# Down-projection of a gated decode kernel with batch rows as outputs: 72 wide matmuls instead of 144 narrow ones, fewer VectorE instructions, last output weights split by columns

## The chip, the cores and the metric

The kernel runs on one core of one Trainium2 chip. The metric is the device time of one execution in microseconds (us).

## The reference

```python
g = sigmoid((x * gate_w).sum(-1))                        # x: 8 x 1 x 576
q = (x @ wq).reshape(8, 1, 32, 128)                      # 32 heads of 128
a = softmax(q . k_cache / sqrt(128)) . v_cache           # caches: 8 x 32 x 4096 x 128
a = a.reshape(8, 1, 4096) @ wo
b = gelu(layernorm(x) @ w1 + b1) @ w2 + b2               # w1: 576 x 4608, w2: 4608 x 576
return g * a + (1 - g) * b                               # everything bf16 in memory
```

The two caches are nearly all of the 557 MB that must be read. The second branch (b) is small, but its weights are read first and it is computed first.

## The kernel before

SBUF has three big slots. The loads go, in order, wq, w1, w2 into slots 0, 1, 2, then K0, K1, V0, K2, V1, K3, V2, ... (8 MB each; a number is a group of 8 heads of one batch row), each into the slot of three loads earlier. A load may therefore be issued only when its slot's previous content has been used: K1 after the up-projection (w1), V0 after the down-projection (w2), K2 after the scores of group 0 (K0), and V1 after the scores of group 1 (K1). All issues come from one queue, in this order.

```python
    def load_kv(kind, g):
        n = n_load[0]; n_load[0] += 1
        s = n % 3
        ...
        land[kind, g] = op("sync", lambda e: e.dma_start(slot[s][:, :, :], src), free[n - 3], dma=dma)

    # down-projection: the 576 output columns as four quarters of 144 at partition offsets 0, 32, 64, 96
    def quarters(lhsT, w, first, stop, waits):
        for i in range(4):
            last = op("tensor", lambda e, i=i: e.matmul(
                y_ps[32 * i:32 * i + B, 0:QN], lhsT=lhsT, rhs=w[:, i * QN:(i + 1) * QN], start=first, stop=stop),
                waits if i == 0 else ())
        return last

    for jt in range(NJ):                                   # NJ = 36 k tiles
        p_down = quarters(hT_sb[:, jt, :], w2_sb[:, jt, :], jt == 0, False, ...)
    for i in range(4):
        p_b2 = ...                                         # (1 - g) * b2, fp32, into the same y_ps
    free[2] = [p_b2]
    ...
    def q_of(g):        # mask q on GpSimd, broadcast it by two matmuls, copy it on ScalarE
    def mult(g, c):     # VectorE: K chunk *= q; then TensorE adds the products up into PSUM
    def scores(g, between):
        mult(g, 0); between(0); mult(g, 1); between(1)
        for c in range(NCK):                               # 8 chunks
            reduce(g, c)                                   # VectorE, from PSUM
            if c + 2 < NCK: mult(g, c + 2); between(c + 2)
```

In TensorE's program the q broadcast of group 0, and with it all scores, stands behind the down-projection (at 59.22 us before the change, behind the last matmuls of that branch at 58.86).

## Time and profile before

| | before |
|---|---|
| median | 1296.31 us (three runs, known when the prediction was made); 1295.85 us with the three runs made beside the changed kernel |
| mean read rate | 431 GB/s |
| DMA queue q1, share of the 16 engines' span | 99.6% |
| TensorE, VectorE, ScalarE busy | 57%, 63%, 12% |

From the page of the kernel before: the busy time of each engine over the span, the read rate in 40 equal slices of the span, and the main DMA queue.

```profile
PE 733.4 (57%) x4926; PEld 337.1 (26%) x4926; DVE 819.7 (63%) x873; ACT 161.0 (12%) x587; POOL 40.4 (3%) x60
GB/s 406 427 447 424 439 430 436 432 430 436 434 428 436 436 432 438 430 438 432 430 436 434 428 436 438 430 438 430 438 430 432 436 432 434 432 438 430 436 424 366
q1 hardware_dynamic: 10528, 556.94, 99.6%
```

No engine is near full; the reads are at nearly the same rate, 424 to 447 GB/s, in every slice but the first and the last. The kernel is a stream of loads, and an engine matters only where it lets that stream run dry, or after the last landing.

The timeline of the kernel before, cut to what gates the early loads. Columns: start and length in us, engine, line, operation, what it writes and reads, count, and in brackets the idle time before it and what ended it. SL is the memory of the slots and all that is cut from them, PS is PSUM. SPq rows are the load issues.

```profile
42.96 0.33 SPq L384 DMA_DIRECT2D SL<-in_A_k_cache_dram  x1
...
54.97 3.96 PE L544 MATMUL PS<-SL 128*8 128x144 bf16 x144 [2.07 <-DVE SL L538]
58.86 0.43 PE L553 MATMUL PS<-SL,diag 8*8 8x144 f32 x8
59.22 0.25 PE L569 MATMUL PS<-Qm,Sel 128*64 128x128 bf16 x2
59.34 0.33 SPq L384 DMA_DIRECT2D SL<-in_A_v_cache_dram  x1
...
59.89 4.49 DVE L580 TENSOR_TENSOR SL<-SL,q_bc 128x4096 bf16<-128x4096 bf16 x2 [5.06 <-DMA SL<-in_A_k_cache_dram]
...
84.42 0.33 SPq L384 DMA_DIRECT2D SL<-in_A_k_cache_dram  x1
...
111.47 0.33 SPq L384 DMA_DIRECT2D SL<-in_A_v_cache_dram  x1
```

Read downward: 144 matmuls in 3.96 us, 27 ns each (a sign of overlap: the 384-column matmuls of the up-projection, one after another, start 163 ns apart at the full clock, which is 61 ns for 144 columns; the profile also records the clock that TensorE is granted, here 0.5 or 1.0 of full speed, "cold" and "warm" in the prediction), then b2, then the q broadcast, then the first score multiply at 59.89 us. The issues are K1, V0, K2 and V1. The packet records of the same trace say when the DMA engines need them: an 8 MB load occupies the engines for 19.35 us, and K2's last packets end between 115.56 and 117.47 us (mean 116.2). V1, issued at 111.47, is thus some 3.7 us ahead of its need, with the time from issue to first packet (about 1 us) taken off. That is the thinnest margin of the kernel: K2, at 84.42, is some 11 us ahead, and by the same sum no later cache load is less than 11 us ahead.

### The profile page before, as it was taken

What the parts mean: (1) busy time and instruction counts of PE and PEld (TensorE: products, weight loads), DVE (VectorE), ACT (ScalarE), POOL (GpSimd) and SP (SyncE); (2) the same over time, 40 slices, a digit from 0 to 9 for tenths busy, and PEclk for the clock granted to TensorE, in tenths of its full rate; (3) what the DMA queues carried; (4) which work ended last, traced back from release to release, by engine and by line L of the source; (5) the groups of instructions that cost most, each with busy time, mean ns of one, the idle gap of its engine ahead of it and who ended that gap; (6) DMA issues with size and microseconds to landing.
All of it is one profiled execution on the core that took longest, in us unless ns stands there. A gap on an engine that the chain in (4) does not pass through costs nothing.

```text
span 1293.2 us, 11790 instructions
## 1 busy us (share of the span) xinstructions
PE 733.4 (57%) x4926; PEld 337.1 (26%) x4926; DVE 819.7 (63%) x873; ACT 161.0 (12%) x587; POOL 40.4 (3%) x60
## 2 busy tenths in 40 slices
PE   3666566555556555556555556555556555556646
PEld 1322223122223222223222223222223222223223
DVE  2387567665567665567665567765567765567762
ACT  1011110111110011110011110011111011111011
POOL 1001000000000000000000000000000000000000
PEclk8799898878898887898787899778888877888888
DMA  9999999999999999999999999999999999999998
GB/s 406 427 447 424 439 430 436 432 430 436 434 428 436 436 432 438 430 438 432 430 436 434 428 436 438 430 438 430 438 430 432 436 432 434 432 438 430 436 424 366
DMA packets 10591, 557.16 MB, mean 431 GB/s; under 512 B 1201, under 2 KB 1233, under 8 KB 1745
## 3 DMA queue, kind: packets, MB, share of 16 engines
q1 hardware_dynamic: 10528, 556.94, 99.6%
q8 instruction: 9, 0.15, 0.0%
q10 hardware_dynamic: 50, 0.04, 0.0%
q14 instruction: 4, 0.03, 0.0%
HBM read 556.96 MB, written 0.01 MB: 431 GB/s over the span
## 4 chain that ended last, share of the span: by engine, by line
DMA 54%; DVE 26%; PE 14%; ACT 5%; issue 1%; SPq 0%; ACTq 0%; DVEq 0%
DMA SL<-in_A_k_cache_dram 50%; DVE SL L580 20%; PE PS L585 7%; DVE s_sb L591 5%; ACT P L625 4%; PE PS L640 4%; DMA SL<-in_B_w_dram 2%; DMA SL<-in_A_wo_dram 2%; PE PS L515 1%; PE PS L656 1%; ACT O_sb L645 1%; PE PS L544 0%; PE PS L518 0%; PE PS L649 0%; PE PS L535 0%
## 5 line engine op out<-in xcount | busy, mean ns | idle before, releaser
L585 PE MATMUL PS<-SL,ident 128*128 128x512 bf16 x2048 | 547.7, 420 | 518.3 <-DVE SL L580 518.3
L580 DVE TENSOR_TENSOR SL<-SL,q_bc 128x4096 bf16<-128x4096 bf16 x256 | 582.0, 2284 | 313.6 <-DMA SL<-in_A_k_cache_dram 313.6
L585 PEld LDWEIGHTS PS<-SL,ident 128*128 128x128 bf16 x2048 | 199.0, 106 | 853.8 <-DVE SL L580 614.8
L591 DVE TENSOR_REDUCE s_sb<-PS 128x32 f32<-128x512 f32 x256 | 175.8, 687 | 90.4 <-PE PS L585 90.3
L625 ACT ACTIVATE P<-s_sb,hb 128x256 bf16<-128x256 f32 x256 | 126.2, 494 | 663.3 <-PE PS L640 645.5
L640 PE MATMUL PS<-SL,P 128*32 128x512 bf16 x2048 | 128.5, 389 | 0.0
L640 PEld LDWEIGHTS PS<-SL,P 128*32 128x32 bf16 x2048 | 96.4, 138 | 17.9 <-issue 3.1
L564 POOL TENSOR_SCALAR Qm<-Q,sel 128x256 bf16<-128x256 bf16 x33 | 33.7, 1020 | 896.6 <-ACT O_sb L645 845.2
L572 ACT ACTIVATE q_bc<-PS 128x128 bf16<-128x128 f32 x33 | 9.1, 277 | 407.4 <-PE PS L569 407.4
L625 ACT ACTIVATION_READ_ACCUMULATOR P<-s_sb,hb 128x1 f32 x256 | 47.7, 186 | 0.0
L656 PE MATMUL PS<-O_sb,selq 128*32 128x128 f32 x256 | 34.2, 278 | 0.7 <-ACT O_sb L645 0.7
L656 PEld LDWEIGHTS PS<-O_sb,selq 128*32 128x32 f32 x256 | 26.0, 113 | 1.4 <-ACT O_sb L645 1.2
L645 ACT ACTIVATE O_sb<-PS 128x512 f32<-128x512 f32 x32 | 18.4, 574 | 10.0 <-PE PS L640 10.0
L523 DVE COPY SL<-PS 104x1152 f32<-104x1152 f32 x1 | 1.4, 1357 | 28.7 <-PE PS L518 28.7
L515 PE MATMUL PS<-SL 128*8 128x384 bf16 x60 | 13.2, 356 | 6.8 <-DMA SL<-in_B_w_dram 6.8
L669 DVE SCALAR_TENSOR_TENSOR On<-PS,rz,dqm 32x128 f32<-32x128 f32 x32 | 10.9, 339 | 9.0 <-PE PS L656 7.9
L683 POOL TENSOR_TENSOR OT<-OTs,g 32x96 bf16<-32x96 f32 (+2 forms) x12 | 4.2, 347 | 320.3 <-DVE OTs L673 320.2
L610 DVE TENSOR_REDUCE mA<-s_sb 128x1 f32<-128x256 f32 x32 | 13.4, 420 | 1.1
L673 DVE TENSOR_REDUCE OTs<-On 32x32 f32<-32x128 f32 x32 | 12.1, 378 | 1.1
L649 PE MATMUL PS<-acc,hsel 128*32 128x8 f32 x64 | 7.4, 188 | 5.9 <-ACT O_sb L645 4.7
L663 DVE TENSOR_REDUCE zs<-PS 32x1 f32<-32x8 f32 x32 | 4.7, 147 | 8.2 <-PE PS L656 7.9
L649 PEld LDWEIGHTS PS<-acc,hsel 128*32 128x32 f32 x64 | 4.5, 110 | 19.5 <-issue 12.7
(82 smaller groups left out, 114.5 us busy)
## 6 DMA issues: line engine op xcount, KB each, us to landing
SL<-in_A_v_cache_dram SPq DMA_DIRECT2D x2, 4096.0 KB, 38.4
SL<-in_B_w_dram SPq DMA_DIRECT2D x1, 5184.0 KB, 37.7
SL<-in_B_w_dram SPq DMA_DIRECT2D x1, 4608.0 KB, 24.1
SL<-in_A_wq_dram SPq DMA_DIRECT2D x1, 4096.0 KB, 13.0
SL<-in_A_wo_dram SPq DMA_DIRECT2D x1, 3456.0 KB, 22.0
SL<-in_A_wo_dram SPq DMA_DIRECT2D x1, 864.0 KB, 23.7
SL<-in_B_w_dram SPq DMA_DIRECT2D x1, 576.0 KB, 25.0
SL<-in_A_wq_dram SPq DMA_DIRECT2D x1, 512.0 KB, 13.6
```

Of the source, the lines that this page charges most:

```text
L515: p_up = op("tensor", lambda e, o=o, r=r, kt=kt, yi=yi: e.matmul(o, lhsT=yT_sb[:, yi, :], rhs=r, start=(kt == 0), stop=False), [v_yT, *ld_ ...
L564: g_qm[g] = op("gpsimd", lambda e: e.tensor_scalar(out=Qm[:, :, :].rearrange("p k d -> p (k d)"), in0=Q4[:, 2 * hg * DH:(2 * hg + 2) * DH] ...
L580: v_mult[g, c] = op("vector", lambda e: e.tensor_tensor(out=part, in0=part, in1=qb, op=ALU.mult), [land["k", g], a_qb[g]], token="tensor" ...
L585: p_sum[g, c] = op("tensor", lambda e, r=r, n=n: e.matmul(tr_ps[par][:, :], lhsT=ident[:, :], rhs=r, start=(n == 0), stop=(n == NCH - 1)), ...
L591: v_red[g, c] = op("vector", lambda e: e.tensor_reduce(out=s_sb[:, c * CT:(c + 1) * CT], in_=tr_ps[par][:, :].rearrange("p (t c) -> p t c" ...
L610: t = op("vector", lambda e: e.tensor_reduce(out=mA[:, 0:1], in_=s_sb[:, :], axis=AX.X, op=ALU.max), [v_red[g, NCK - 1], c_mA], token=own)
L625: a_exp[g] = op("scalar", lambda e, h=h: e.activation(out=P[:, :, h, :], in_=s_sb[:, :].rearrange("p (s t) -> p s t", s=2), func=ACT.Exp, ...
L640: p_pv[g] = op("tensor", lambda e, o=o, lhsT=lhsT, rhs=rhs, tq=tq: e.matmul(o, lhsT=lhsT, rhs=rhs, start=(tq < 4), stop=(tq >= NTQ - 4)), ...
L645: a_ev[g] = op("scalar", lambda e: e.activation(out=O_sb[:].rearrange("p t d -> p (t d)"), in_=o_ps[:, :], func=ACT.Copy), [p_pv[g], p_z.g ...
L649: p_z[g] = op("tensor", lambda e: e.matmul(oz_ps[0:32, DH:DH + HB], lhsT=hsel[:, :], rhs=acc[:, place(g), :], start=True, stop=True), [a_e ...
L656: p_oz[g] = op("tensor", lambda e, tt=tt: e.matmul(oz_ps[0:32, 0:DH], lhsT=selq[:, tt, :], rhs=O_sb[:, tt, :], start=(tt == 0), stop=(tt = ...
L673: v_norm[g] = op("vector", lambda e: e.tensor_reduce(out=OTs[:, :, place(g + 2)], in_=On[:, :].rearrange("p (q j) -> p j q", q=NDQ), axis= ...
```

## The change

Its intent: fewer instructions on TensorE and VectorE, and a shorter end. The down-projection writes the 8 batch rows as one 8 x 576 block, with 512 and 64 columns of w2 moving per k tile; one VectorE instruction of each softmax goes; small copies move from VectorE to ScalarE; the last row of wo comes as two column pieces. The core of the diff (cuts marked):

```diff
+    b_ps = PS[0:B, 5 * 512:5 * 512 + D]
...
     for jt in range(NJ):
-        p_down = quarters(hT_sb[:, jt, :], w2_sb[:, jt, :], jt == 0, False, ...)
+        for n0, n1 in ((0, 512), (512, D)):
+            p_down = op("tensor", lambda e, jt=jt, n0=n0, n1=n1: e.matmul(
+                b_ps[:, n0:n1], lhsT=hT_sb[:, jt, :], rhs=w2_sb[:, jt, n0:n1], start=(jt == 0), stop=(jt == NJ - 1)), ...)
+    v_b = op("vector", ... scalar_tensor_tensor(out=b_sb, in0=b2_8, scalar=1 - g, in1=b_ps, mult, add), [p_down, ld_b2])
     for i in range(4):
-        p_b2 = ... lhsT=diag2[:, 1, :], rhs=b2_f ...
+        p_y = ... lhsT=spread8[:, 0:B], rhs=b_sb[:, i * QN:(i + 1) * QN] ...    # fp32, spreads the rows to the quarters
...
-        t = op("vector", ... mC = -gm ...)
-        t = op("vector", ... transpose(mD, mC))
+        t = op("vector", ... transpose(mD, gmb))           # sign put into the next instruction
...
-    WO = ((0, 24), (24, 30), (30, 32))
+    WO = ((0, 24, 0, 4), (24, 31, 0, 4), (31, 32, 2, 4), (31, 32, 0, 2))
```

More of the change, by code (lines that the diff above doesn't have):

```diff
@@ L268, in bass_gated_mix__mha_block_cached__mixer_channel_mlp__decode_kernel @@
     b2_8 = late.take([B, D])
-    b2_f = late.take32([B, D])
+    b_sb = late.take32([B, D])
     t2 = late.take32([128, FC])
@@ L276, in bass_gated_mix__mha_block_cached__mixer_channel_mlp__decode_kernel @@
     zs = sb("zs", [32, 1], F32)
+    rz = sb("rz", [32, 1], F32)
     acc = sb("acc", [128, GL, HB], F32)
@@ L288, in bass_gated_mix__mha_block_cached__mixer_channel_mlp__decode_kernel @@
     one1 = sb("one1", [1, B], BF16)
-    diag2 = sb("diag2", [B, 2, B], F32)
+    diag = sb("diag", [B, B], F32)
     g4 = sb("g4", [128, 2], F32)
-    g32 = sb("g32", [32, 2, B], F32)
+    g32 = sb("g32", [32, B], F32)
     ident = sb("ident", [128, 128], BF16)
-    hneg = sb("hneg", [128, HB], F32)
+    hpos = sb("hpos", [128, HB], F32)
     sel32 = sb("sel32", [128, HB, TQ], F32)
@@ L298, in bass_gated_mix__mha_block_cached__mixer_channel_mlp__decode_kernel @@
     mB = sb("mB", [128, 32], F32)
-    mC = sb("mC", [128, 32], F32)
     mD = sb("mD", [128, 32], F32)
@@ L304, in bass_gated_mix__mha_block_cached__mixer_channel_mlp__decode_kernel @@
     O_sb = sb("O_sb", [128, TQ, DH], F32)
-    rz = sb("rz", [128, 1], F32)
     PS = nc.alloc_psum_tensor("PS", [128, 8 * 512], F32)
@@ L316, in bass_gated_mix__mha_block_cached__mixer_channel_mlp__decode_kernel @@
     g4_ps = bank[3][:, 0:2]
-    g32_ps = bank[3][0:32, 64:64 + 2 * B]
+    g32_ps = bank[3][0:32, 64:64 + B]
     ht_ps = PS[:, 0:NJ * 32].rearrange("p (j c b) -> p j c b", j=NJ, c=4)
+    b_ps = PS[0:B, 5 * 512:5 * 512 + D]
     xt_ps = bank[7]
@@ L405, in bass_gated_mix__mha_block_cached__mixer_channel_mlp__decode_kernel @@
                                                     base=PH - 1, pattern=[[PH, HB], [0, NDQ]], channel_multiplier=-1), [t])
-    c_hneg = op("vector", lambda e: e.tensor_scalar(out=hneg[:, :], in0=hsel[:, ::NDQ], scalar1=-1.0, scalar2=60000.0,
+    c_hpos = op("vector", lambda e: e.tensor_scalar(out=hpos[:, :], in0=hsel[:, ::NDQ], scalar1=-1.0, scalar2=-60000.0,
                                                     op0=ALU.add, op1=ALU.mult), [c_hsel])
@@ L416, in bass_gated_mix__mha_block_cached__mixer_channel_mlp__decode_kernel @@
         axis=AX.X, op=ALU.add), [c_id])
-    c_selq = op("vector", lambda e: e.tensor_copy(
+    c_selq = op("scalar", lambda e: e.copy(
         out=selq[:].rearrange("p t (h q) -> p t h q", q=NDQ),
@@ L421, in bass_gated_mix__mha_block_cached__mixer_channel_mlp__decode_kernel @@
     c_one1 = memset("gpsimd", one1[:], 1.0)
-    c_b2 = op("gpsimd", lambda e: e.tensor_copy(out=b2_f, in_=b2_8), [ld_b2])
-    c_sp8 = op("vector", lambda e: e.tensor_copy(
+    c_sp8 = op("scalar", lambda e: e.copy(
         out=spread8[:].rearrange("b (c r) -> b c r", c=4),
@@ L427, in bass_gated_mix__mha_block_cached__mixer_channel_mlp__decode_kernel @@
         out=Rows[:], in_=ident[:, :].rearrange("p (h r) -> p h r", h=4), axis=AX.X, op=ALU.add), [c_id])
-    c_Sel = op("vector", lambda e: e.tensor_copy(
+    c_Sel = op("scalar", lambda e: e.copy(
         out=Sel[:].rearrange("p (h r) -> p h r", h=4),
@@ L465, in untransposed @@
     def untransposed(dst, col, waits):
-        return op("vector", lambda e: e.tensor_copy(
+        return op("scalar", lambda e: e.copy(
             out=dst.rearrange("p k b -> p (k b)"), in_=xt_ps[:, col:col + (NKF + 2) * B]), waits)
@@ L476, in bass_gated_mix__mha_block_cached__mixer_channel_mlp__decode_kernel @@
                                                    scalar1=-1.0, scalar2=1.0, op0=ALU.mult, op1=ALU.add), [a_g])
-    v_dg = op("vector", lambda e: e.tensor_tensor(
-        out=diag2[:], in0=bass.AP(tensor=ident, offset=0, ap=[[pstride(ident), B], [0, 2], [1, B]]),
-        in1=bass.AP(tensor=stat, offset=G_COL, ap=[[pstride(stat), B], [1, 2], [0, B]]), op=ALU.mult), [v_omg, c_id])
+    v_dg = op("vector", lambda e: e.tensor_scalar(
+        out=diag[:, :], in0=ident[0:B, 0:B], scalar1=stat[:, G_COL:G_COL + 1], scalar2=None, op0=ALU.mult), [v_omg, c_id])
     v_yz = spread(yz, y_sb, [v_y])
@@ L484, in bass_gated_mix__mha_block_cached__mixer_channel_mlp__decode_kernel @@
            [v_dg, c_sp8])
-    t = op("tensor", lambda e: e.matmul(g32_ps, lhsT=ones8[:, :], rhs=diag2[:].rearrange("k s b -> k (s b)"),
+    t = op("tensor", lambda e: e.matmul(g32_ps, lhsT=ones8[:, :], rhs=diag[:, :],
                                         start=True, stop=True), [c_one8])
-    v_g4 = op("vector", lambda e: e.tensor_copy(out=g4[:, :], in_=g4_ps), [t])
-    v_g32 = op("vector", lambda e: e.tensor_copy(out=g32[:].rearrange("p s b -> p (s b)"), in_=g32_ps), [t])
+    v_g4 = op("scalar", lambda e: e.copy(out=g4[:, :], in_=g4_ps), [t])
+    v_g32 = op("scalar", lambda e: e.copy(out=g32[:, :], in_=g32_ps), [t])
     a_Q = []
@@ L539, in bass_gated_mix__mha_block_cached__mixer_channel_mlp__decode_kernel @@
         out=hT_sb[32 * c:32 * c + 32, :, :], in_=ht_ps[0:32, :, c, :]), [p_hT]) for c in range(4)]
-    def quarters(lhsT, w, first, stop, waits):
-        for i in range(4):
-            last = op("tensor", lambda e, i=i: e.matmul(
-                y_ps[32 * i:32 * i + B, 0:QN], lhsT=lhsT, rhs=w[:, i * QN:(i + 1) * QN], start=first, stop=stop),
-                waits if i == 0 else ())
-        return last
-    for jt in range(NJ):
-        p_down = quarters(hT_sb[:, jt, :], w2_sb[:, jt, :], jt == 0, False,
-                          [ld_w2, *v_hT, v_yT] if jt == 0 else ())
+    for jt in range(NJ):
+        for n0, n1 in ((0, 512), (512, D)):
+            p_down = op("tensor", lambda e, jt=jt, n0=n0, n1=n1: e.matmul(
+                b_ps[:, n0:n1], lhsT=hT_sb[:, jt, :], rhs=w2_sb[:, jt, n0:n1], start=(jt == 0), stop=(jt == NJ - 1)),
+                [ld_w2, *v_hT] if jt == n0 == 0 else ())
+    v_b = op("vector", lambda e: e.scalar_tensor_tensor(
+        out=b_sb, in0=b2_8, scalar=stat[:, OMG_COL:OMG_COL + 1], in1=b_ps, op0=ALU.mult, op1=ALU.add), [p_down, ld_b2])
     for i in range(4):
-        p_b2 = op("tensor", lambda e, i=i: e.matmul(
-            y_ps[32 * i:32 * i + B, 0:QN], lhsT=diag2[:, 1, :], rhs=b2_f[:, i * QN:(i + 1) * QN], start=False, stop=False),
-            [c_b2, v_dg])
-    free[2] = [p_b2]
+        p_y = op("tensor", lambda e, i=i: e.matmul(
+            y_ps[32 * i:32 * i + B, 0:QN], lhsT=spread8[:, 0:B], rhs=b_sb[:, i * QN:(i + 1) * QN], start=True, stop=False),
+            [v_b, v_yT])
+    free[2] = [p_y]
     a_qb, v_mult, v_red, p_sum, v_nm, a_exp, p_pv, a_ev, p_z, p_oz, v_norm, g_ot, g_qm, p_q, v_rz = ({} for _ in range(15))
@@ L615, in softmax @@
         gmb = bass.AP(tensor=gm, offset=0, ap=[[pstride(gm), 128], [1, 2], [0, PH]])
-        t = op("vector", lambda e: e.tensor_scalar(out=mC[:, :].rearrange("p (k r) -> p k r", k=2), in0=gmb,
-                                                   scalar1=-1.0, scalar2=None, op0=ALU.mult), [t], token=own)
-        t = op("vector", lambda e: e.transpose(mD[:, :], mC[:, :]), [t], token=own)
-        v_nm[g] = op("vector", lambda e: e.tensor_scalar(out=hb8[:, :], in0=hneg[:, :], scalar1=mD[:, 0:1], scalar2=None,
-                                                         op0=ALU.add), [t, c_hneg, a_exp.get(g - 1)],
+        t = op("vector", lambda e: e.transpose(mD[:, :], gmb), [t], token=own)
+        v_nm[g] = op("vector", lambda e: e.tensor_scalar(out=hb8[:, :], in0=hpos[:, :], scalar1=mD[:, 0:1], scalar2=-1.0,
+                                                         op0=ALU.add, op1=ALU.mult), [t, c_hpos, a_exp.get(g - 1)],
                      token="scalar" if in_loop(g) else None)
@@ L711, in load_wo @@
         w = A_wo.rearrange("(p j) n -> p j n", j=NJO)
-        for n, (j0, j1) in enumerate(WO):
-            t = load("sync", wo_sb[:, j0:j1, :], w[:, j0:j1, :], f"ld_wo{n}", waits)
-            ld_wo.update({j: t for j in range(j0, j1)})
+        for n, (j0, j1, i0, i1) in enumerate(WO):
+            cols = slice(i0 * QN, i1 * QN)
+            t = load("sync", wo_sb[:, j0:j1, cols], w[:, j0:j1, cols], f"ld_wo{n}", waits)
+            ld_wo.update({(j, i): t for j in range(j0, j1) for i in range(i0, i1)})
     for g in range(NG):
@@ L758, in bass_gated_mix__mha_block_cached__mixer_channel_mlp__decode_kernel @@
     place_o("vector", last - 1, last + 1)
+    p_a = {}
     for j in range(NJO):
-        p_a = quarters(OT[:, j, :], wo_sb[:, j, :], False, j == NJO - 1, [ld_wo[j], *g_ot.values()])
-    parts = [op("vector" if i < 2 else "scalar", lambda e, i=i: (e.tensor_copy if i < 2 else e.copy)(
-        out_sb[:, i * QN:(i + 1) * QN], y_ps[32 * i:32 * i + B, 0:QN]), [p_a]) for i in range(4)]
+        for i in range(4) if j < NJO - 1 else (2, 3, 0, 1):
+            p_a[i] = op("tensor", lambda e, i=i, j=j: e.matmul(
+                y_ps[32 * i:32 * i + B, 0:QN], lhsT=OT[:, j, :], rhs=wo_sb[:, j, i * QN:(i + 1) * QN], start=False,
+                stop=(j == NJO - 1)), [ld_wo[j, i], *g_ot.values()])
+    parts = [op("vector" if i % 2 == 0 else "scalar", lambda e, i=i: (e.tensor_copy if i % 2 == 0 else e.copy)(
+        out_sb[:, i * QN:(i + 1) * QN], y_ps[32 * i:32 * i + B, 0:QN]), [p_a[i]]) for i in (2, 3, 0, 1)]
     ld_out = [load("sync", out_flat, out_sb[:, :], "ld_out", parts)]
```

## The prediction

> **What bounds the kernel.** The transfers. The queue table gives q1 99.6% of the 16 DMA engines' span; the table of 40 slices shows DMA at 9 everywhere and 424 to 439 GB/s from slice 3 to slice 39. TensorE is 57% busy, VectorE 63%. In the packet times an 8 MB cache load takes 19.35 us, and from 1.8 us to the last weight piece (1289.7 us) no moment is without packets in flight. So nothing on an engine counts unless it delays an issue until the queue runs dry, or lies after the last landing.
>
> **Loop.** Per group two loads take 38.7 us, while VectorE needs about 25. The change drops one VectorE instruction per softmax (0.18 us plus a gap): some 0.22 us x 32, all inside slack. Worth about 0.
>
> **Prologue.** Constants and small copies move from VectorE to ScalarE; they end before wq lands (the timeline has the first Q matmul at 14.99 us, waiting for it). Worth 0.
>
> **Down-projection: the one step with a cost.** Before, the 144 matmuls (8x144 outputs at four partition offsets) run four at a time: the timeline has them from 54.97 to 58.9 us, four per 120 ns, at granted clock 0.5 until 58.2. After, 72 matmuls (512 and 64 columns) all write at partition 0, so I expect no overlap between them. The Trainium skill, "TensorE: Matmul & The Clock Gate" (Back-to-back issue gap), gives N/1.2 ns per matmul at the low clock and N/2.4 + 2.5 at the full one; this trace agrees: the up-projection's 384-column matmuls start 320 ns apart cold, 163 ns warm. Estimate: per k tile 480 ns cold, 245 ns warm; about 3.3 us cold (7 tiles), then 29 warm: down-projection ends near 65.5 instead of 58.9. Then a VectorE add (about 0.75, estimated from the 8x576 reductions at 0.73), four fp32 matmuls (0.43 measured for their like). The first q broadcast and the first scores start near 67.4 instead of 59.89: a delay of about 7.5 us. About 0.5 comes back on the first chunk, 0.2 in softmax.
>
> **Does that dry the queue?** V0's issue (59.34) becomes about 67, needed by about 75.5: fine. K2's issue (84.42) becomes about 91, needed by about 95: just fine. V1's issue waits for the second group's scores: 111.47 becomes about 118. The DMA engines finish K2 between 115.56 and 117.47 (mean 116.15), and the first packet comes about 1 us after an issue (0.79 to 1.83 at the start). So I expect a hole of about 3 us near 116 to 119 us, in which the DMA engines idle. It is not won back, since transfers bound everything after; by K3 the slack is restored.
>
> **End.** Last piece split by columns: packets of 576 B instead of 2304 (93 ns; about 30 ns estimated). The second piece grows from 24 to 28 matmuls (about 23 ns each), so the output chain gains only 0.1 to 0.4 us.
>
> **Predicted:** 1296.3 + 3.0 - 0.2, about 1299.0 us; 8 in 10 between 1296.0 and 1301.5. Faster by over 2%: 0.005; within 2%: 0.985; slower by over 2%: 0.01.
>
> **What would show it.** Timeline: 72 matmuls lasting 9 to 12 us; first score multiply at 66 to 69. Windows: DMA share down for about 3 us near 117, nowhere else. In the chain of waits the first K issue and its DMA piece start later. Last landing to end of span: about 0.2 shorter than before's 3.0 us. VectorE busy down about 6 us without any effect.
>
> **What would make it wrong.** The matmuls overlapping more than I think, or warming earlier (delay under 4 us: no hole, time about 1296); cold longer (hole of 5 us); issue-to-packet latency hidden; run-to-run spread of 1.6 us, as large as half the effect.

## The result

The changed kernel takes 1301.36 us (six runs, 1300.21 to 1303.81) against 1295.85 us (six runs, 1295.15 to 1296.80): 5.5 us more. The ratio is 1.0043, 95% interval 1.0031 to 1.0056: within 2%, and clearly slower. (Ratios are the mean time of one kernel's fast runs over that of the other's of the same rounds, so not quite the ratio of the medians.)

The page of the changed kernel, the lines shown before:

```profile
PE 743.8 (57%) x4854; PEld 338.4 (26%) x4854; DVE 813.8 (63%) x835; ACT 163.6 (13%) x595; POOL 36.6 (3%) x59
GB/s 411 436 430 360 418 447 426 434 432 432 440 428 444 424 442 428 432 438 428 444 424 442 428 436 434 428 444 426 442 428 434 434 430 440 428 440 430 434 425 357
q1 hardware_dynamic: 10672, 556.94, 99.2%
```

VectorE has 38 instructions and 5.9 us of work less, TensorE 72 matmuls less, and the time is longer. The rate shows why: the fourth slice (97.5 to 130 us) has 360 GB/s where the kernel before had 424. The timeline of the changed kernel, as above:

```profile
43.77 0.33 SPq L384 DMA_DIRECT2D SL<-in_A_k_cache_dram  x1
...
55.78 11.01 PE L541 MATMUL PS<-SL 128*8 128x512 bf16 x72 [2.07 <-DVE SL L536]
66.83 0.80 DVE L544 SCALAR_TENSOR_TENSOR SL<-SL,stat,PS 8x576 f32<-8x576 bf16 x1 [11.19 <-PE PS L541]
67.69 0.43 PE L547 MATMUL PS<-SL,spread 8*8 8x144 f32 x8 [0.90 <-DVE SL L544]
...
68.17 0.33 SPq L384 DMA_DIRECT2D SL<-in_A_v_cache_dram  x1
...
68.71 4.50 DVE L574 TENSOR_TENSOR SL<-SL,q_bc 128x4096 bf16<-128x4096 bf16 x2 [1.08 <-ACT q_bc L566]
...
93.74 0.33 SPq L384 DMA_DIRECT2D SL<-in_A_k_cache_dram  x1
...
120.30 0.33 SPq L384 DMA_DIRECT2D SL<-in_A_v_cache_dram  x1
```

The down-projection went from 3.96 to 11.01 us, the first multiply from 59.89 to 68.71, V1's issue from 111.47 to 120.30 us: after K2 was done. Of the 8.8 us by which the first multiply is later, 7.05 are these matmuls, 0.96 the add and the spreading behind them, and 0.81 a later end of the up-projection, which the change doesn't touch. In the table of windows the fields are the stretch, its length, the busy time of five engines, then the clock that TensorE was granted, the DMA engines' share and GB/s. First the kernel before, then the changed one:

```profile
110.00:115.00 5.00, 5.00 (x71) 2.87 (x69) 2.21 (x8) 0.00 (x0) 0.00 (x0) 1.00 0.97 419
115.00:120.00 5.00, 0.05 (x4) 0.00 (x0) 2.06 (x1) 4.52 (x17) 0.23 (x1) 0.97 1.08 462
120.00:125.00 5.00, 4.72 (x16) 1.82 (x16) 3.85 (x4) 0.00 (x0) 3.14 (x1) 0.69 0.97 419
```

```profile
110.00:115.00 5.00, 3.77 (x16) 1.37 (x16) 5.00 (x4) 0.00 (x0) 0.00 (x0) 1.00 1.02 436
115.00:120.00 5.00, 3.53 (x16) 1.40 (x16) 3.91 (x4) 0.00 (x0) 0.00 (x0) 1.00 0.03 13
120.00:125.00 5.00, 4.16 (x68) 2.51 (x67) 4.52 (x8) 1.00 (x5) 0.00 (x0) 1.00 1.10 419
```

For 5 us the DMA engines do nothing (share 0.03, 13 GB/s). The packet records put numbers to it. Call the *hole* the mean time per engine between its last packet of one load and its first of the next. Between K2 and V1 it is 5.1 us here and none before, and no other boundary among the early loads has any. The first packet of each engine after the hole takes 2.8 to 3.4 us instead of 2.42, about 0.7 us more. And from the first load after the hole on, the slowest engine trails the mean of the 16 by about 1.5 us, where in later loads of the kernel before it trails by 0.9: some 0.6 us. (That this lag comes from the hole is not shown: by the same count it is 0.8 and 1.1 us in the traces of runs 1 and 11 and 2.3 in that of run 5, where the hole is 0.1 us at most.) The sum, 5.1 + 0.7 + 0.6, is the 6.4 us by which the last weight packet of this execution is later (1296.13 against 1289.69 us); the medians, over all executions, are 5.5 us apart.

The end gained nothing. First the kernel before, then the changed one, from the second wo piece's landing on:

```profile
1289.46 0.55 PE L544 MATMUL PS<-SL,OT 128*8 128x144 bf16 x24 [0.43 <-DMA SL<-in_A_wo_dram]
1290.22 0.30 PE L544 MATMUL PS<-SL,OT 128*8 128x144 bf16 x8 [0.21 <-DMA SL<-in_A_wo_dram]
1290.57 0.63 DVE L761 CAST out_sb<-PS 8x144 bf16<-8x144 f32 x2 [3.50 <-PE PS L544]
1291.23 0.37 SPq L326 DMA_DIRECT2D out_dram<-out_sb  x1
```

```profile
1296.21 0.67 PE L755 MATMUL PS<-SL,OT 128*8 128x144 bf16 x32 [0.77 <-DMA SL<-in_A_wo_dram]
1296.92 0.63 DVE L758 CAST out_sb<-PS 8x144 bf16<-8x144 f32 x2 [4.03 <-PE PS L755]
1297.61 0.37 SPq L326 DMA_DIRECT2D out_dram<-out_sb  x1
```

The second wo piece is now larger (28 matmuls wait for it instead of 24), so the 4 matmuls of the small column pieces run straight behind them and all copies start together. From the last weight packet to the end of the span it is 3.58 us, before 3.48. Up to the issue of the output it is 1.48, before 1.55; the output's own write, which the change leaves alone, then took 2.10 against 1.93.

### The profile page after: what moved, and what is told of

It is laid out like the page before. It is cut to its first block, busy times and chain, and to the rows that moved or that the text cites. A ratio compares the mean times of both kernels' runs of the same rounds, so it can differ in the third digit from the quotient of the medians.

```text
span 1299.7 us, 11618 instructions
## 1 busy us (share of the span) xinstructions
PE 743.8 (57%) x4854; PEld 338.4 (26%) x4854; DVE 813.8 (63%) x835; ACT 163.6 (13%) x595; POOL 36.6 (3%) x59
## 4 chain that ended last, share of the span: by engine, by line
DMA 53%; DVE 25%; PE 15%; ACT 5%; issue 1%; SPq 0%; ACTq 0%; DVEq 0%
DMA SL<-in_A_k_cache_dram 49%; DVE SL L574 20%; PE PS L579 8%; DVE s_sb L585 5%; ACT P L617 4%; PE PS L632 4%; DMA SL<-in_B_w_dram 2%; DMA SL<-in_A_wo_dram 2%; PE PS L513 1%; PE PS L648 1%; PE PS L541 1%; ACT O_sb L637 1%; PE PS L516 0%; PE PS L641 0%; PE PS L533 0%
## 5 line engine op out<-in xcount | busy, mean ns | idle before, releaser
L558 POOL TENSOR_SCALAR Qm<-Q,sel 128x256 bf16<-128x256 bf16 x33 | 30.5, 924 | 919.0 <-ACT O_sb L637 845.8
L541 PE MATMUL PS<-SL 128*8 128x512 bf16 x72 | 11.0, 322 | 2.1 <-DVE SL L536 2.1
```

The lines of the kernel that those rows point to most:

```text
L541: p_down = op("tensor", lambda e, jt=jt, n0=n0, n1=n1: e.matmul(b_ps[:, n0:n1], lhsT=hT_sb[:, jt, :], rhs=w2_sb[:, jt, n0:n1], start=(jt = ...
L558: g_qm[g] = op("gpsimd", lambda e: e.tensor_scalar(out=Qm[:, :, :].rearrange("p k d -> p (k d)"), in0=Q4[:, 2 * hg * DH:(2 * hg + 2) * DH] ...
```

## The experiments

The theory: the new matmuls all write at partition offset 0 and so don't overlap; the down-projection holds back the first scores, these V1's issue, and the stream runs dry once. Rivals: another part of the change costs the time; late compute costs by itself; the wide moving side is slow wherever it writes.

The numbers of all runs, from their traces (one execution each) and their timed executions. "First multiply" and "V1 issued" are from the timeline, "hole" (K2 to V1) from the packet records as above; "before" is the kernel before in the same rounds.

| run | first multiply | V1 issued | hole | median, range | before, median |
|---|---|---|---|---|---|
| before | 59.89 | 111.47 | 0 | 1295.85 (1295.15 to 1296.80) | - |
| changed | 68.71 | 120.30 | 5.1 | 1301.36 (1300.21 to 1303.81) | 1295.85 |
| 1 e1_old_down | 61.16 | 112.50 | 0.1 | 1296.03 (1295.37 to 1297.16) | 1295.26 |
| 2 e2_new_down_only | 70.05 | 122.03 | 6.4 | 1300.88 (1300.25 to 1303.42) | 1295.26 |
| 3 e3_split_v1 | 71.55 | 111.69 (half) | 0 | 1295.49 (1294.71 to 1296.51) | 1295.26 |
| 4 e4_col_groups | 60.31 | 112.06 | 0 | 1297.32 (1295.21 to 1297.79) | 1295.26 |
| 5 d12_extra | 62.72 | 113.85 | 0.1 | 1296.56 (1295.00 to 1297.68) | 1295.94 |
| 6 d26_extra | 68.27 | 118.59 | 3.7 | 1299.05 (1298.29 to 1301.49) | 1295.94 |
| 7 d40_extra | 70.21 | 120.59 | 5.5 | 1302.21 (1300.43 to 1303.30) | 1295.94 |
| 8 e5_warm | 65.00 | 115.33 | 0.6 | 1296.87 (1296.63 to 1297.30) | 1295.94 |
| 9 f1_before_split | 64.17 | 104.73 (half) | 0 | 1295.10 (1295.07 to 1295.75) | 1296.38 |
| 10 f2_best | 59.62 | 99.76 (half) | 0 | 1294.97 (1294.93 to 1295.11) | 1296.38 |
| 11 f1_again | 61.22 | 101.78 (half) | 0 | 1295.34 (1295.18 to 1295.72) | 1295.31 |
| 12 f2_again | 60.04 | 100.17 (half) | 0 | 1295.05 (1294.85 to 1295.73) | 1295.31 |

All outputs are right.

### 1. The change with the old down-projection

```diff
-        for n0, n1 in ((0, 512), (512, D)):
-            p_down = ... b_ps[:, n0:n1] ...
-    v_b = ...
+        p_down = quarters(hT_sb[:, jt, :], w2_sb[:, jt, :], jt == 0, False, ...)
+    for i in range(4): p_b2 = ... lhsT=diagb[:, :], rhs=b2_f[:, i * QN:(i + 1) * QN] ...
```

> The changed kernel with the old down-projection (144 matmuls at four partition offsets) put back; all else of the change stays. Theory (the cost is the slower down-projection, which issues the load V1 too late): down-projection about 4 us, V1 issued at 111 to 113 us, no hole in the DMA packets near 117, median about 1295.8 us, the same as before within 1 us. Rival (the cost comes from the copies moved to ScalarE, the leaner softmax or the 576-byte packets at the end): still about 1301 us.

Measured: ratio 1.0004 (0.9991 to 1.0018), V1 issued at 112.50 us, no hole. The rest of the change, the copies, the shorter softmax and the split end, costs nothing that can be seen, and gains nothing either.

### 2. The kernel before with the new down-projection alone

The same edit on the other kernel, the other way round.

> The kernel before with the new down-projection alone. Theory: about 11 us of down-projection, V1 issued at 119 to 121 us, a hole of 4 to 6 us, median about 1301.3 us. Rival (the other parts cost it): about 1296 us.

Measured: ratio 1.0040 (1.0026 to 1.0054), V1 issued at 122.03 us, hole 6.4 us, 10.54 us of down-projection. V1 and the hole lie beyond what was expected: the profiled execution was the slowest of the five (1303.42 us), with an up-projection that ended 2.6 us later than in the trace of before; K2 too was late enough in it to leave 0.3 us. Runs 1 and 2 together put the whole loss on this one part.

### 3. The changed kernel with V1 in two halves

K1's first four score chunks free the first half of its slot 11 us before the last one does, so the first half of V1 may be issued then:

```diff
+        if (kind, g) == ("v", 1):
+            op("sync", lambda e: e.dma_start(slot[s][:, 0:half, :], src[:, 0:half, :]), [p_sum[1, 3]], dma=...)
+            t = op("sync", lambda e: e.dma_start(slot[s][:, half:, :], src[:, half:, :]), free[n - 3], dma=...)
```

> The changed kernel, with V1 loaded as two halves; the first half waits only for the first four of the second group's eight score chunks, the second half for all, as before. The down-projection stays slow. Theory: the first half is issued near 109 us, the DMA engines go from K2 to V1 without a hole, median about 1296 us though the scores are as late as in the changed kernel (first multiply near 68 us). Rival (the time is lost to compute that is late, or to the tail, and the hole is only a sign of it): about 1301 us.

Measured: ratio 0.9997 (0.9984 to 1.0011). The issues in its timeline (K1, V0, K2, and the two halves of V1):

```profile
46.50 0.33 SPq L394 DMA_DIRECT2D SL<-in_A_k_cache_dram  x1
71.01 0.33 SPq L394 DMA_DIRECT2D SL<-in_A_v_cache_dram  x1
96.01 0.33 SPq L394 DMA_DIRECT2D SL<-in_A_k_cache_dram  x1
111.69 0.33 SPq L381 DMA_DIRECT2D SL<-in_A_v_cache_dram  x1
122.89 0.33 SPq L384 DMA_DIRECT2D SL<-in_A_v_cache_dram  x1
```

In this execution the scores were later than in the changed kernel's (first multiply at 71.55 us, expected near 68, so that the first half came at 111.69 and not near 109), and K2, issued at 96.01, already left a hole of 0.7 us behind V0. Yet the whole 5 us were back. Late compute by itself costs nothing; the late issue does.

### 4. The new matmuls over four partition offsets

Each offset sums a quarter of the k tiles; fp32 matmuls with a selection matrix add the four up.

```diff
-                b_ps[:, n0:n1], lhsT=hT_sb[:, jt, :], ...
+                b4_ps[32 * c:32 * c + B, n0:n1], lhsT=hT_sb[:, 4 * jq + c, :], ...   # c = 0..3
```

> The changed kernel, its 72 matmuls of 512 and 64 columns spread over the partition offsets 0, 32, 64, 96 (each sums a quarter of the k tiles), the four sums added by fp32 matmuls. Theory (all at one offset leaves no overlap): 4 to 5.5 us of down-projection instead of 11, V1 issued at 111.5 to 114 us, hole 0 to 1 us, median 1296 to 1297 us. Rival (w2 as a wide moving side is slow whatever the offset): still about 11 us and about 1301 us.

Measured, the same 72 matmuls in the timelines, first of the changed kernel's down-projection alone put into the kernel before (run 2), then of this run:

```profile
57.59 10.54 PE L551 MATMUL PS<-SL 128*8 128x512 bf16 x72 [2.07 <-DVE SL L538]
```

```profile
54.57 3.83 PE L554 MATMUL PS<-SL 128*8 128x512 bf16 x72 [1.47 <-DVE SL L542]
```

Same shapes, same count, 3.83 us instead of 10.54: it is the common offset that costs, not the width. Nor is it that one matmul adds to the result of the last: in the changed kernel the 512 and the 64 columns go to different places in PSUM at one offset, and the starts still lie 410 and 70 ns apart at clock 0.5, 216 and 29 at 1.0. At equal clock the gain is fourfold: about 480 ns (clock 0.5) or 245 ns (1.0) serve one k tile at one offset and four k tiles at four. The two lengths above show less because the longer run spends some 70% of its time at clock 1.0, the shorter one only its last 0.8 us. The hole is gone. The median of 1297.32 is 2 us above that of before in these rounds, but the ratio of 1.0011 has an interval (0.9998 to 1.0025) that includes 1, and the profiled execution has the span of before (1293.4 us); whether something of it is real stays open.

### 5 to 7. The kernel before with needless matmuls ahead of the first scores

12, 26 and 40 matmuls of 512 columns on constants, writing to a PSUM bank that nobody reads, between the down-projection and the first q broadcast. V0's issue doesn't wait for them.

```diff
+    for _ in range(26):
+        op("tensor", lambda e: e.matmul(bank[5][0:B, :], lhsT=ident[:, 0:B], rhs=<ident, four times>, ...), [v_h])
     q_of(0)
```

> The kernel before, with 12 needless 512-column matmuls on TensorE between the down-projection and the first q broadcast: nothing else is late than the first scores. Theory (V1 must be issued about 1 us before the DMA engines finish K2, near 115.2 us; before issues it near 111.5 to 112.5, so some 3 us are slack): the extra 2.6 to 4 us move V1's issue to 114 to 116 us, hole 0 to 1 us, median within 1 us of before. Rival (any delay of the first scores costs its own length): about 3 us slower.

> As the run with 12, with 26 needless matmuls (5.6 to 7 us). Theory: V1 issued at 117 to 119 us, hole 2 to 4 us plus a restart of 0.7, median 1298 to 1300 us. Rival (each microsecond of delay costs one): 5.6 to 7 us slower, 1301 to 1302.5.

> As the run with 12, with 40 needless matmuls (8.6 to 10 us): about the delay of the changed kernel, with the old down-projection. Theory: V1 issued at 120 to 122 us, hole 5 to 6.5 us, median 1301 to 1302.5 us, like the changed kernel. Rival 1 (the delay costs its length): 1304 to 1305.5. Rival 2 (it was the new matmuls' own traffic or placement, not lateness): no slower than before.

Measured: ratios 1.0005 (0.9991 to 1.0019), 1.0029 (1.0015 to 1.0043) and 1.0051 (1.0037 to 1.0065). With 40, the needless matmuls and V1's issue:

```profile
60.81 8.80 PE L696 MATMUL PS<-ident 128*8 128x512 bf16 x40
...
120.59 0.33 SPq L384 DMA_DIRECT2D SL<-in_A_v_cache_dram  x1
```

The 40 took 8.80 us and the first multiply came 10.3 us later than in the profile of before, but the median rose by 6.3 us; 26 gave 3.1 us, 12 gave 0.6 us. So there is a threshold: the delay is free as long as V1 is issued in time, and then costs about its length. A kernel with the old down-projection and 40 idle matmuls behaves like the changed one. In all five traces with a hole, the first V1 packet came 0.94 to 0.96 us after the start of the issue. At the edge the loss is not quite zero: with V1 at 113.85 us (12 matmuls) the hole is only 0.1 us, but the load still took 0.7 us longer than usual, with packets of up to 4.1 us at its start; and in this trace one engine ended the next load 1.5 us behind all others, so that the last weight packet came 1.9 us later than in the trace of before (the medians are 0.6 us apart).

### 8. The changed kernel with TensorE kept busy

```diff
+    keep_warm(28, ...)      # behind the Q projection
+    keep_warm(33, ...)      # behind the up-projection
+    keep_warm(7, ...)       # ahead of the down-projection
+    keep_warm(9, ...)       # ahead of the first scores' sums
```

> The changed kernel with needless matmuls in TensorE's idle stretches from 20 to 71 us (28 before the up-projection, 33 and 7 before the down-projection, 9 before the first scores), so that the granted clock stays at 1.0. Theory (some 2 us of the delay beyond my estimate, and its scatter from run to run, come from how long the clock stays at 0.5 in these stretches): up-projection about 14 us instead of 16.4, down-projection about 9 us instead of 11, V1 issued at 113 to 116 us instead of 120.3, hole 0 to 1.5 us, median 1295.5 to 1297.5 us. Rival (the clock has little part, the columns decide): V1 at 119 or later, about 1301 us.

Measured: ratio 1.0009 (0.9996 to 1.0023), median 1296.87. The granted clock of the changed kernel was 0.5 from 22.4 to 32.7, from 46.3 to 60.0 and from 70.2 to 77.0 us (clock records of its trace); here only from 50.8 to 54.3. Its down-projection:

```profile
53.94 9.14 PE L550 MATMUL PS<-SL 128*8 128x512 bf16 x72
```

Needless work on TensorE leaves 0.9 us of the 5.5 (medians, each against before of its own rounds): V1's issue moved from 120.30 to 115.33. Its five executions lie within 0.7 us, the six of the changed kernel within 3.6. A likely reason is the clock: the moment at which it goes up differs from execution to execution (the end of the up-projection lies between 42.5 and 46.7 us in the traces of all the other runs, whose up-projection is the same), and without slack a later V1 is a later end. That is not shown: the timed executions have no traces, and the kernel before, with its slack, scatters by 2.5 to 3.0 us in the rounds of the twelve runs.

### 9 to 12. Can either kernel be beaten?

Run 9 is the kernel before with V1 in two halves. Run 10 is the changed kernel with the old down-projection, V1 in two halves and a last wo piece of two rows by columns. Runs 11 and 12 repeat them.

```diff
-    WO = ((0, 24, 0, 4), (24, 31, 0, 4), (31, 32, 2, 4), (31, 32, 0, 2))
+    WO = ((0, 24, 0, 4), (24, 30, 0, 4), (30, 32, 2, 4), (30, 32, 0, 2))     # runs 10 and 12 only
```

> The kernel before, with V1 loaded as two halves (the first waits for four of the second group's eight score chunks). Theory (before has slack at this point, and no hole): median within 0.7 us of before, spread about the same. Rival (part of before's time and spread of 2 to 3 us are small holes at V1): median 0.7 us or more lower, spread smaller.

> The changed kernel with the old down-projection, V1 in two halves, and a last wo piece of two rows split by columns (the piece ahead of it back to six rows): what should be best of the change. Theory: no hole, tail after the last weight packet 3.3 us against 3.5 before; median within 0.7 us of before, at best 0.2 us lower, not clear of noise.

> The kernel before with V1 in two halves, once more, since the first time it spread 0.7 us where before spread 3.0. If before's slow executions are ones in which the phase of the clock makes V1 late: again under 1 us of spread, and no execution slower than 1296.0 us, while before's nine again reach 1297 us or more. If it was chance: executions of 1296.5 us or more here too.

> The best version once more, for the same question: spread under 1 us and a median of 1294.7 to 1295.4 us if the split load takes away small holes; 1295.5 to 1296.5 with executions above 1296.5 us if the first result was chance.

Measured: ratios 0.9994 (0.9980 to 1.0007), 0.9992 (0.9978 to 1.0006), 1.0001 (0.9987 to 1.0014), 0.9998 (0.9985 to 1.0012). The first round put the medians 1.3 and 1.4 us below before's, as the rival of run 9 has it; the repeat put them at 0.0 and 0.3, with ratios of 1 within their intervals all four times. So no version is faster than before by anything that these rounds resolve. What repeats is the scatter: the 20 executions of the two versions lie between 1294.85 and 1295.75 us, the 18 of before beside them between 1294.55 and 1297.62. That fits with small holes at V1 in some executions of the kernel before, but a timed execution leaves no trace, so it is not shown. And run 3 with the same split reached 1296.51 (in its profiled execution, another one, K2 came late). In the traces of runs 9 to 12 the end after the last weight packet takes 3.78, 2.96, 3.68 and 3.78 us: too scattered for any verdict on the 0.2 us hoped for from the pieces of wo.

## Why the prediction came out as it did

- **"The transfers" bound the kernel, and only a dry queue counts: right.** Runs 3 and 5 delay compute by up to 12 us with no or little effect on the time.
- **Loop and prologue worth about 0: right.** 5.9 us of VectorE work less gained nothing (run 1: ratio 1.0004).
- **No overlap at one partition offset: right.** 11.01 us against 3.96; run 4 shows that the offset is the cause.
- **Which load: right.** V0 (68.17) and K2 (93.74, 1.9 us ahead of its need) still came in time, V1 did not; the only hole lies at 116.3 to 121.4 us.
- **Size of the hole, "about 3 us": too small; this is the term of the sum that was mis-sized.** It was 5.1 us, and the cost with it 5.5 instead of 2.8 us: the measured 1301.36 lies only 0.14 us inside the stated range. The prediction had named the case ("cold longer (hole of 5 us)") without counting on it. It had V1's issue at 118 us; it came at 120.30. The pieces, each against the step as predicted: the up-projection ended 0.8 us later than in the trace of before, a matter of the clock's phase that the prediction took over unchanged; the clock stayed at 0.5 until 59.95 us, not 58.2, so the down-projection took 11.0 instead of about 10.5 us; and group 0's scores, said to win back "about 0.5" on the first chunk, took 0.5 us longer than before (25.03 us from first multiply to K2's issue, against 24.53). The clock falls to 0.5 around TensorE's 2.8 us pause ahead of them in both traces, but stays there for 6.8 us here and for 3.4 before. The second group won back some 0.3 us more than the 0.2 foreseen (26.56 us from K2's issue to V1's, against 27.05). Run 8 shows that this clock part matters: without it V1 comes at 115.33. The prediction's "first packet about 1 us after an issue" was right (0.95).
- **What the prediction left out:** the slow first packets after a hole (0.7 us) and, in the profiled execution, the lag of the slowest engine (0.6 us).
- **End, gain of 0.1 to 0.4 us: not seen.** 3.58 against 3.48 us in one trace each, within the scatter of the ends (2.96 and 3.78 in two traces of one kernel, runs 10 and 12). The part that the pieces of wo bear on, up to the issue of the output, got 0.07 us shorter; the rest is the output's write.

## What to carry to other kernels

In a kernel that is bound by loads, find for every load how long before its need it is issued; the smallest of these margins says how much compute may be slowed for nothing, and beyond it each microsecond of delay cost about one. Count a matmul's cost with its overlap: four narrow outputs at four partition offsets beat one wide output at one offset, though the instructions are twice as many. Where a margin is thin, issue the load in parts, each as soon as its part of the buffer is free.

## What the Trainium skill lacked or had wrong

- "DMA: Bandwidth & Descriptors", Specifications, gives a first-byte latency of about 0.6 us for loads issued from the sync engine. In five traces with dry engines the first packet came 0.94 to 0.96 us after the start of the 0.33 us issue record, so 0.62 us after its end: the two agree if the issue itself is added, which the page doesn't say. That after such a pause each engine's first 64 KB packet takes 2.8 to 3.4 us instead of 2.42 (changed kernel) stands nowhere there.
- "TensorE: Matmul & The Clock Gate", Part 3, Measured speedup, states the gain of three column tiles (2.38 times) for 512 columns. It has no measured one for four column tiles. For a full accumulation over 36 k tiles at four offsets this case shows 3.83 us against 10.54 for 72 matmuls of 512 and 64 columns, 2.8 times, both beginning at the low clock, and four times at equal clock (run 4).
- The same page, Part 1, holds the cost of the warm-up for under 1% of a typical kernel. That is so here too (some 4.6 us of 1301), but it doesn't say that the time at the low clock can also decide whether a load is issued in time: keeping the clock up left 0.9 of the 5.5 us (run 8).
- No page that was read says how to find the margin with which a load is issued ahead of its need: here 3.7 us at V1, and some 11 us at the next thinnest.
